# Attention and two MLPs on one core: order of the first weights' loads, sizes of two chunks, time of the second weights' conversion

## Chip, core and metric

The kernel runs on one core of a Trainium2 chip. The metric is the device time of one execution in microseconds. The kernel before takes 964.87 us, the median of three runs from 963.07 to 965.61.

## What is computed

Attention with a few global tokens, and two MLPs behind it, all in float32 as far as the outputs go; the four weight matrices arrive as float64. In short:

```python
k_all = np.concatenate([k_g, k_l], axis=2);  v_all = np.concatenate([v_g, v_l], axis=2)
out_g = np.matmul(sm(scale * np.matmul(q_g, k_all.transpose(0, 1, 3, 2))), v_all)
s_ll  = np.where(np.abs(pos[:, None] - pos[None, :]) <= 32, scale * q_l @ k_l.T, -1e9)
a_l   = sm(np.concatenate([scale * q_l @ k_g.T, s_ll], axis=-1))
out_l = np.matmul(a_l, v_all)
x = np.concatenate([out_g, out_l], axis=2)     # 4 x 8 heads x (32 + 512) x 64 -> (2176, 512)
h = x @ w_in;  g = np.maximum(0.01 * h, h);  x = g @ w_out        # d_ff = 2048
h = x @ w_in2; g = h - np.tanh(h);           out = g @ w_out2     # d_ff = 2048
```

## The kernel before

**Tiles.** The 2176 tokens are cut into five chunks: 512, 512, 512, 256, and 256 with the 128 global tokens (384). An item is one block of 128 of the 2048 hidden features (f, 16 of them) for one chunk. In an item of the first MLP, `mlp1_a` makes h in 12 matmuls, ACT and DVE turn it into g, cut in a high and a low part, and `mlp1_b` adds g's product with the second weights to four PSUM banks (y0 to y3) in 12 more, two items later (`SKEW`). Weights and activations are split so (high, low), and three products replace one.

**Order of items.** n = 0 to 7: chunk 0, f = 0 to 7. n = 8 to 23: chunk 1. n = 24 to 31: chunk 0, f = 8 to 15. n = 32 to 47: chunk 2. n = 48 to 63: chunk 3. n = 64 on: chunk 4, and from about 80 the second MLP, chunk by chunk in `order2`. Since chunk 0 is done in two halves, its partial y goes to DRAM (`yp_dram`) after the first half, is loaded by `y_part` into columns of `xh` and `xl` that are free then, and is added when y leaves PSUM in `mlp1_y`.

**Attention** is cut into 32 steps (one pair of heads of 256 tokens); stage s makes the keys of step s + 1, the scores and softmax of s, transposes s - 1 and multiplies s - 2 by v. Ten stages run before item 0. The others are spread beside items by the table in the main loop (last stage, first and last item): stages 10 to 17 beside n = 0 to 7, 18 to 25 beside 24 to 31, 26 to 29 beside 32 to 47, 30 to 33 beside 48 to 58. A chunk's tokens must have left attention before its first item. k and q are loaded for two steps at a time, a group (`load_kq`, three buffers), and so is v (`load_v`, two buffers); global queries add some work every fourth stage (`gavps`, `vn`, `vg`).

**Weights.** They arrive as float64. `load_w` loads a block (512 KB), `convert_w` makes float32 of it with one ACT operation (L127) and three of DVE, and `split_w` makes the high and low parts. For the first MLP's w_in the raw block has a place of its own (`in_load`, then `in_job`): six loads are traced in the first part, the rest beside n = 0 to 9. w_out goes through two buffers (`out_load`, `out_job`), is stored split in DRAM and fetched again for each chunk (`wo_fetch`, two transfers of 256 KB an item). The second MLP's weights are loaded through the same two raw buffers, converted into one of two buffers `wf`, and stored in DRAM as float32 (`w2_job`, 33 of them for 32 blocks); `w2_at` says beside which item each is due, from `w2_first` = 25 to 47. They come back beside chunk 4.

**What sets the order.** PE's instructions keep the order of the program up to item 78 (`fix`). On the other engines and on the DMA queues a planner puts instructions where it expects them to be ready, by the program's order among those that are. Nearly all DMAs are issued from SP's queue, in one line: an instruction there that waits for a buffer holds back those behind it. ACT and DVE too take their work in line. `tc.issue_after(x)` makes what is traced inside it follow x, where it is on x's own engine or queue, and does nothing else.

Of the kernel before, what the change touches and what calls it, by code (L numbers as in the profile page):

```python
# [21 lines left out]
def kernel(  # L22
# [14 lines left out]
    nc = tc.nc  # L37
# [6 lines left out]
    NF = DFF // 128  # L44
# [5 lines left out]
    NU = NHV * H  # L50
# [26 lines left out]
    xh = [persist.tile([128, ND, n], F32R, name=f"xh{n}") for n in (512, 640)]  # L77
    xl = [persist.tile([128, ND, n], F32R, name=f"xl{n}") for n in (512, 640)]
    ident = persist.tile([128, 128], F32, name="ident")

    yp_dram = dram.tile([128, ND, 512], F32, name="yp")
# [2 lines left out]
    w2i_dram = [dram.tile([128, DM], F32, name=f"w2id{f}") for f in range(NF)]  # L84
    w2o_dram = [dram.tile([128, DM], F32, name=f"w2od{f}") for f in range(NF)]

    halves = [2, 2, 2, 1, 1]
    sizes = [256 * n for n in halves]
    starts = [sum(sizes[:c]) for c in range(5)]
    sizes[4] += B * SG  # L90
    order2 = [0, 1, 2, 4, 3]

    place = [(0, 0), (1, 0), (1, 0), (0, 0), (1, 256)]

    def f32(t):
        return t.bitcast(F32)
# [6 lines left out]
    def load_w(kind, w, f, raw=None):  # L103
        if raw is None:
            raw = mlp.tile([128, DM, 2], I32, tag="wraw", name="wraw", bufs=2)
        wi = w.bitcast(I32)
        if kind == "in":
            src = wi[:, f * 256 : (f + 1) * 256].rearrange("(k p) f -> p k f", p=128)
            dst = raw.rearrange("p (k n) t -> p k (n t)", k=ND)
        else:  # L110
            src = wi[f * 128 : (f + 1) * 128, :]
            dst = raw.rearrange("p n t -> p (n t)")
        nc.sync.dma_start(out=dst, in_=src)
        return raw
# [49 lines left out]
    y_ps = {}  # L164
    anchor = [None]
    last_av = [None]
    last_exp = [None]
    av_n = []

    def mm1(xh_t, xl_t, N, tag="h"):  # L170
# [41 lines left out]
    HF = NF // 2  # L212
# [5 lines left out]
        return f // HF * HF + HF - 1 if c == 0 else NF - 1  # L218

    def y_part():  # L220
        for k, x in enumerate((xh[0], xl[0])):
            nc.sync.dma_start(out=f32(x)[:, :, 256:], in_=yp_dram[:, :, 256 * k : 256 * k + 256])

    def mlp1_b(c, f):
        N = sizes[c]
# [17 lines left out]
    def mlp1_y(c, f):  # L243
        N = sizes[c]
        if f == y_last(c, f):
            for d in range(ND):
                st = mlp.tile([128, 512], F32, tag="yst", name="yst", bufs=2)
                if c == 0 and f == NF - 1:
                    for k, x in enumerate((xh[0], xl[0])):
                        ks = slice(256 * k, 256 * k + 256)  # L250
                        nc.vector.tensor_add(st[:, ks], y_ps[d][:, ks], f32(x)[:, d, 256:])  # L251
                elif d % 2:
                    nc.scalar.activation(st[:, :N], y_ps[d][:, :N], AF.Copy)
                else:
                    nc.vector.tensor_copy(st[:, :N], y_ps[d][:, :N])
                to = yp_dram if f < NF - 1 else y_dram[c]
                nc.sync.dma_start(out=to[:, d, :N], in_=st[:, :N])
# [61 lines left out]
    def load_kq(g):  # L319

        if g >= NU // 4:
            return
        b, a, hs = place_of(g)
        qr = att.tile([128, 2, 4, D], F32, tag="qr", name="qr", bufs=3)
        kr = att.tile([128, 3, 4, D], F32, tag="kr", name="kr", bufs=3)

        keyed(kr, k_l, k_g, b, a, hs, [nc.sync, nc.sync, nc.scalar] if g == 0 else None)
        queue = nc.scalar if g < 2 else nc.sync
        for t in range(2):
            s0 = a * HALF + t * 128  # L330
            queue.dma_start(out=qr[:, t], in_=q_l[b, hs, s0 : s0 + 128, :].rearrange("h s d -> s h d"))
        for k in range(2):
            h2 = slice(2 * k, 2 * k + 2)
            raw_t[2 * g + k] = qr[:, :, h2, :], kr[:, :, h2, :]
# [369 lines left out]
    def in_load():  # L704
        if in_todo:
            f = in_todo.pop(0)
            place = persist.tile([128, DM, 2], I32, tag=f"win{f}", name=f"inraw{f}")
            in_raw.append((f, load_w("in", w1_in, f, place)))

    def out_load():  # L710
        if out_todo:
# [57 lines left out]
        tc.cur_priority = at + max(tc.cur_priority - max(at - n, 0), 0)  # L769

    gtodo = []
    w2_first = 25

    start_tags = ["att0", "att1", "att2", "y0", "y1", "y2", "y3"]
    run_tags = ["att0", "att1", "att2"]
# [74 lines left out]
    if True:  # L850
# [16 lines left out]
        for pp in range(PRE):  # L867
            for op in stage(pp):
                op()
            if pp % 2 == 0:  # L870
                in_load()
            if pp == 0:
                load_kq(2)
            if pp == 1:
                load_v(1)
            if pp >= 2 and pp % 2 == 0:
                in_job()
            if pp == PRE - 2:
                out_load()
                out_load()  # L880
# [9 lines left out]

        beside = {}
        pp = PRE
        for last, n0, n1 in ((17, 0, HF - 1), (25, 3 * HF, 4 * HF - 1), (29, 2 * NF, 3 * NF - 1), (NU // 2 + 1, 3 * NF, 4 * NF - 6)):
            ops = []
            while pp <= last:
                ops += stage(pp)
                pp += 1
            for k, op in enumerate(ops):
                beside.setdefault(n0 + k * (n1 - n0) // len(ops), []).append(op)
# [3 lines left out]
            items.insert(n1 - 2 + 1 + 2 * k, items.pop(n1 + k))  # L903
        w2_at = {}
        for k in range(2 * NF + 1):
            w2_at.setdefault(w2_first + k * (47 - w2_first) // (2 * NF), []).append(k)
        last0 = 9 * NF
        b_at = {}
        for n, (ph, c, f) in enumerate(items):
# [2 lines left out]
        for n in range(len(items) + 8):  # L912
            ph, c, f = items[n] if n < len(items) else (3, 0, 0)
            one = items[n - 1] if 0 < n <= len(items) else (3, 0, 0)
            if ph == 1:
                if n in (0, 2, 4, 6) or HF <= n < 2 * HF:
                    in_job()
                if n < 2 * HF - 2:
                    in_load()
                if 1 <= n <= HF or 2 * HF + 1 <= n <= 3 * HF:  # L920
                    out_job()
                if n == 4 * HF:
                    y_part()
                if c == 4 and f == 0:
                    while gtodo:
# [88 lines left out]
```

## Time and profile before

| | us |
|---|---|
| median of three runs | 964.87 |
| profiled execution | 965.56 |
| its span | 963.8 |
| PE busy | 925.9 |
| DVE busy | 624.5 |
| ACT busy | 536.9 |

The page gives each engine's busy time and, in 40 slices of the span, its busy share in tenths, with PE's granted clock (9 is nearly the full 2.4 GHz; the other level is half of it). A window is a stretch of the span with the busy time of each engine in it. In a timeline, a bracket tells how long the engine was idle before an instruction, and whose end released it. A group gathers instructions of one line and form. "DMA share" is the mean busy share of the core's 16 DMA engines. Digits in names are left out: in_moe_w_in_dram is the w_in of either MLP; loaded as inraw it is the first's, as wraw the second's.

### The profile page before, as it was taken

How to read it: one execution, taken by the hardware profiler on the slowest of the kernel's cores; microseconds unless marked ns; L12 is line 12 of the kernel's file. 1: busy time of each engine (PE TensorE's matmuls, PEld its weight loads, DVE VectorE, ACT ScalarE, POOL GpSimd, SP SyncE). 2: the span in 40 equal slices, each digit the busy share in tenths (PEclk: the TensorE clock that was granted, in tenths of full speed). 3: DMA queues.
4: the chain of work that ended last, by engine and by line, in shares of the span. 5: the costliest groups of instructions: out<-in, count | busy, mean ns of one | idle time of the engine just before them, and what ended most of it. 6: DMA issues, size and time to landing. Idle time of an engine off the chain costs nothing.

```text
span 963.8 us, 15440 instructions
## 1 busy us (share of the span) xinstructions
PE 925.9 (96%) x5436; PEld 771.4 (80%) x5436; DVE 624.5 (65%) x1373; ACT 536.9 (56%) x1223; POOL 36.9 (4%) x67
## 2 busy tenths in 40 slices
PE   7869999999998989999999999999999999999998
PEld 4657778788776767777899999888888888899997
DVE  3864878544564454555313347988888988888886
ACT  5866775443666444444434347656555655655565
POOL 5400000000000000000000000000000000000022
PEclk9998999999999999999999999999999999999999
DMA  7897567445476786787647675001100100010010
GB/s 184 240 278 177 152 187 218 149 167 161 126 212 174 224 280 206 251 254 249 194 143 259 192 235 169 29 1 34 45 1 0 46 21 1 1 45 1 1 34 23
DMA packets 146574, 129.22 MB, mean 134 GB/s; under 512 B 89280, under 2 KB 108736, under 8 KB 146496
## 3 DMA queue, kind: packets, MB, share of 16 engines
q1 hardware_dynamic: 143840, 127.57, 43.7%
q10 hardware_dynamic: 2656, 0.66, 0.3%
q8 instruction: 43, 0.70, 0.3%
q14 instruction: 35, 0.29, 0.1%
HBM read 101.45 MB, written 26.74 MB: 133 GB/s over the span
## 4 chain that ended last, share of the span: by engine, by line
PE 77%; DMA 10%; ACT 4%; DVE 4%; SPq 2%; issue 2%; POOL 0%; ACTq 0%; DVEq 0%
PE h L55 34%; PE o L55 19%; PE y L55 14%; DMA wraw<-in_moe_w_in_dram 3%; PE sps L55 2%; PE ptps L453 2%; PE avps L55 2%; ACT e L423 2%; DMA w2id<-wf 2%; DMA wraw<-in_moe_w_out_dram 2%; PE gavps L55 1%; DMA w2od<-wf 1%; ACT wf L127 1%; PE sgps L55 1%; PE kps L354 1%
## 5 line engine op out<-in xcount | busy, mean ns | idle before, releaser
L55 PE MATMUL h<-xh,win 128*128 128x512 f32 (+2 forms) x1280 | 359.3, 364 | 3.6 <-ACT g L204 3.5
L55 PEld LDWEIGHTS h<-xh,win 128*128 128x128 f32 x1280 | 229.2, 190 | 40.1 <-ACT g L204 6.2
L55 PE MATMUL h<-xl,win 128*128 128x512 f32 (+2 forms) x640 | 230.0, 359 | 0.0
L55 PEld LDWEIGHTS h<-xl,win 128*128 128x128 f32 x640 | 121.3, 190 | 15.7
L55 PE MATMUL y<-gh,woh 128*128 128x512 f32 (+2 forms) x320 | 121.4, 379 | 5.1 <-DVE yst L251 3.7
L206 DVE TENSOR_TENSOR gl<-g,gh 128x512 fp32r<-128x512 f32 (+2 forms) x80 | 48.8, 610 | 114.2 <-ACT gh L205 114.1
L55 PE MATMUL y<-gh,wol 128*128 128x512 f32 (+2 forms) x320 | 115.1, 360 | 0.0
L55 PE MATMUL y<-gl,woh 128*128 128x512 f32 (+2 forms) x320 | 114.4, 361 | 0.0
L55 PE MATMUL o<-wo2l,gh 128*128 128x512 f32 x255 | 99.6, 391 | 0.0
L55 PE MATMUL o<-wo2h,gh 128*128 128x512 f32 x255 | 99.4, 390 | 0.0
L55 PE MATMUL o<-wo2h,gl 128*128 128x512 f32 x255 | 97.7, 390 | 0.0
L633 ACT ACTIVATE u<-h 128x512 f32<-128x512 f32 (+2 forms) x80 | 42.6, 532 | 93.3 <-PE h L55 86.4
L204 ACT ACTIVATE g<-h 128x512 f32<-128x512 f32 (+2 forms) x80 | 42.1, 527 | 60.7 <-PE h L55 60.3
L55 PEld LDWEIGHTS y<-gh,woh 128*128 128x128 f32 x320 | 60.5, 189 | 17.0 <-issue 8.8
L127 ACT ACTIVATE wf<-wraw 128x512 f32<-128x512 f32 x48 | 31.8, 662 | 66.0 <-DMA wraw<-in_moe_w_in_dram 20.6
L658 ACT ACTIVATE gh<-p 128x512 fp32r<-128x512 f32 (+2 forms) x80 | 45.4, 568 | 41.0 <-DVE p L642 41.0
L55 PEld LDWEIGHTS y<-gl,woh 128*128 128x128 f32 x320 | 60.5, 189 | 8.2
L55 PEld LDWEIGHTS y<-gh,wol 128*128 128x128 f32 x320 | 60.8, 190 | 5.7
L639 ACT ACTIVATE u<-u,consts 128x512 f32<-128x512 f32 (+2 forms) x80 | 52.7, 659 | 6.8 <-DVE p L637 4.2
L55 PEld LDWEIGHTS o<-wo2h,gl 128*128 128x128 f32 x255 | 47.9, 188 | 10.1
L659 DVE TENSOR_TENSOR gl<-p,gh 128x512 fp32r<-128x512 f32 (+1 forms) x64 | 41.8, 653 | 21.7 <-ACT gh L658 20.8
L55 PEld LDWEIGHTS o<-wo2h,gh 128*128 128x128 f32 x255 | 47.9, 188 | 9.1
(109 smaller groups left out, 1428.7 us busy)
## 6 DMA issues: line engine op xcount, KB each, us to landing
wraw<-in_moe_w_out_dram SPq DMA_DIRECT2D x32, 512.0 KB, 4.2
woh<-wod SPq DMA_DIRECT2D x64, 256.0 KB, 4.0
wol<-wod SPq DMA_DIRECT2D x64, 256.0 KB, 3.6
inraw<-in_moe_w_in_dram SPq DMA_DIRECT2D x16, 512.0 KB, 6.2
wraw<-in_moe_w_in_dram SPq DMA_DIRECT2D x16, 512.0 KB, 4.8
vr<-in_v_l_dram SPq DMA_DIRECT2D x48, 96.0 KB, 2.8
kr<-in_k_l_dram SPq DMA_DIRECT2D x47, 96.0 KB, 2.9
vn<-in_v_l_dram SPq DMA_DIRECT2D x32, 128.0 KB, 3.3
```

Source lines behind the costliest of these rows:

```text
L55: nc.tensor.matmul(o, lhsT, rhs, start=start, stop=stop)
L127: nc.scalar.activation(w, hw.bitcast(F32), AF.Copy, scale=REBIAS)
L204: nc.scalar.activation(g[:, :N], h[:, :N], AF.Prelu, alpha=0.01)
L206: anchor[0] = nc.vector.tensor_sub(gl[:, :N], g[:, :N], f32(gh)[:, :N])
L354: nc.tensor.transpose(ps[:, c : c + n], kr[:n, t].rearrange("p h d -> p (h d)"), ident[:n, :n])
L423: last_exp[0] = nc.scalar.activation(e[:, h, j, s0 : s0 + n], x, AF.Exp, bias=st[:, k : k + 1], scale=-1.0, accum_out=st[:, 4 + k : 5 + k],)
L453: nc.tensor.transpose(ps[:, k * 128 : (k + 1) * 128], e[:, h, j, c0 : c0 + 128], ident)
L633: nc.scalar.activation(u, h, AF.Square)
L639: nc.scalar.activation(u, u, AF.Square, bias=tc_a2)
L658: nc.scalar.activation(gh[:, :N], p, AF.Copy)
L659: eng["pool" if i == order2[-1] else "dve"].tensor_sub(gl[:, :N], p, f32(gh)[:, :N])
```

## The change

Chunk 2 gets 256 tokens and chunk 3 gets 512; `order2` follows, so that the second MLP still ends with the 256-token chunk. The partial y of chunk 0 is loaded into `xh[1]` and `xl[1]` (columns 256 to 511, which chunk 2 no longer uses) at n = 25, not into `xh[0]` and `xl[0]` at n = 32. Stages 18 to 21 alone stand beside n = 24 to 31, and 22 to 29 beside n = 32 to 47. Each load of w_in follows, on SP, the last q load traced before it (`last_kq`); in the first part they are traced after odd stages instead of even ones, later beside n = 0, 2 and 4 to 11 instead of 0 to 9. The second weights are due from n = 32 to 60 instead of 25 to 47.

```diff
-    halves = [2, 2, 2, 1, 1]
+    halves = [2, 2, 1, 2, 1]
-    order2 = [0, 1, 2, 4, 3]
+    order2 = [0, 1, 3, 4, 2]
+    last_kq = [None]
     def y_part():
-        for k, x in enumerate((xh[0], xl[0])):
-            nc.sync.dma_start(out=f32(x)[:, :, 256:], in_=yp_dram[:, :, 256 * k : 256 * k + 256])
+        for k, x in enumerate((xh[1], xl[1])):
+            nc.sync.dma_start(out=f32(x)[:, :, 256:512], in_=yp_dram[:, :, 256 * k : 256 * k + 256])
...
-                    for k, x in enumerate((xh[0], xl[0])):
+                    for k, x in enumerate((xh[1], xl[1])):
                         ks = slice(256 * k, 256 * k + 256)
-                        nc.vector.tensor_add(st[:, ks], y_ps[d][:, ks], f32(x)[:, d, 256:])
+                        nc.vector.tensor_add(st[:, ks], y_ps[d][:, ks], f32(x)[:, d, 256:512])
...
-            queue.dma_start(out=qr[:, t], in_=q_l[b, hs, s0 : s0 + 128, :].rearrange("h s d -> s h d"))
+            last_kq[0] = queue.dma_start(out=qr[:, t], in_=q_l[b, hs, s0 : s0 + 128, :].rearrange("h s d -> s h d"))
...
-            in_raw.append((f, load_w("in", w1_in, f, place)))
+            with tc.issue_after(last_kq[0].ins):
+                in_raw.append((f, load_w("in", w1_in, f, place)))
...
-    w2_first = 25
+    w2_first = 32
...
-            if pp % 2 == 0:
+            if pp % 2:
                 in_load()
...
-        for last, n0, n1 in ((17, 0, HF - 1), (25, 3 * HF, 4 * HF - 1), (29, 2 * NF, 3 * NF - 1), (NU // 2 + 1, 3 * NF, 4 * NF - 6)):
+        for last, n0, n1 in ((17, 0, HF - 1), (21, 3 * HF, 4 * HF - 1), (29, 2 * NF, 3 * NF - 1), (NU // 2 + 1, 3 * NF, 4 * NF - 6)):
...
-            w2_at.setdefault(w2_first + k * (47 - w2_first) // (2 * NF), []).append(k)
+            w2_at.setdefault(w2_first + k * (60 - w2_first) // (2 * NF), []).append(k)
...
-                if n < 2 * HF - 2:
+                if n in (0, 2) or 4 <= n < 12:
                     in_load()
...
-                if n == 4 * HF:
+                if n == 3 * HF + 1:
                     y_part()
```

## Rows read from the trace of the kernel before

**Rows 1.** The page: span, PE's sum, PE and its clock in 40 slices of 24.1 us.

```profile
span 963.8 us, 15440 instructions
...
PE 925.9 (96%) x5436; PEld 771.4 (80%) x5436; DVE 624.5 (65%) x1373; ACT 536.9 (56%) x1223; POOL 36.9 (4%) x67
...
PE   7869999999998989999999999999999999999998
...
PEclk9998999999999999999999999999999999999999
```

**Rows 2.** Windows (from:to us): length, then busy us of each engine, clock, DMA share, GB/s.

```profile
core 0: us, PE busy (x) PEld busy (x) DVE busy (x) ACT busy (x) POOL busy (x), PEclk, DMA share, GB/s
59.70:81.10 21.40, 12.72 (x103) 9.95 (x101) 10.21 (x32) 11.46 (x32) 0.00 (x0) 0.76 0.84 236
81.10:152.30 71.20, 70.51 (x522) 53.53 (x521) 54.09 (x169) 54.22 (x148) 0.30 (x2) 1.00 0.68 183
176.40:236.20 59.80, 59.80 (x265) 49.55 (x264) 26.98 (x44) 22.49 (x37) 0.00 (x0) 1.00 0.51 167
241.70:334.20 92.50, 86.95 (x603) 65.72 (x602) 47.75 (x169) 54.78 (x153) 0.31 (x2) 0.96 0.63 182
285.60:334.20 48.60, 43.50 (x306) 33.62 (x306) 24.34 (x82) 26.48 (x73) 0.00 (x0) 0.93 0.65 194
334.20:349.40 15.20, 15.20 (x105) 12.02 (x104) 10.22 (x29) 7.33 (x19) 0.00 (x0) 1.00 0.88 283
349.40:367.30 17.90, 14.17 (x62) 11.30 (x61) 7.84 (x17) 6.41 (x13) 0.00 (x0) 0.90 0.79 249
367.30:450.10 82.80, 79.81 (x409) 61.85 (x407) 44.97 (x109) 36.11 (x82) 0.30 (x2) 1.00 0.75 241
334.20:450.10 115.90, 109.19 (x573) 85.17 (x571) 63.03 (x155) 49.85 (x112) 0.30 (x2) 0.99 0.78 247
503.70:512.40 8.70, 8.70 (x75) 8.70 (x74) 2.52 (x5) 2.92 (x7) 0.00 (x0) 1.00 0.66 212
```

**Rows 3.** Timeline of SP's queue around item 0 (start us, us, engine line op tiles).

```profile
50.66 3.84 SPq L113 DMA_DIRECT2D inraw<-in_moe_w_in_dram  x5
...
55.87 5.76 SPq L113 DMA_DIRECT2D inraw<-in_moe_w_in_dram  x5
...
61.72 1.22 SPq L315 DMA_DIRECT2D vr<-in_v_l_dram  x1
```

**Rows 4.** Timeline of PE around item 0; in brackets idle us before and its releaser.

```profile
56.95 0.94 PE L55 MATMUL avps<-pt,vr 128*64 128x128 f32 x16
...
70.19 2.05 PE L55 MATMUL avps<-pt,vr 128*64 128x128 f32 x16 [4.65 <-DMA vr<-in_v_g_dram]
...
75.48 0.42 PE L55 MATMUL gavps<-pg,vg 32*64 32x32 f32 x4 [1.49 <-DMA vg<-in_v_g_dram]
```

**Rows 5.** The same of DVE.

```profile
68.64 1.04 DVE L442 TENSOR_SCALAR e<-e,st 128x192 f32<-128x192 f32 x4
```

**Rows 6.** Timelines of PE and ACT in items 28 to 35: instructions that waited.

```profile
293.33 1.56 PE L55 MATMUL sps<-kt,qt 64*128 64x224 f32 x8 [1.49 <-ACT kt L356]
...
313.04 0.66 PE L453 MATMUL ptps<-ident,e 128*128 128x128 f32 x4 [1.32 <-DVE xl L485]
...
325.16 1.12 PE L453 MATMUL ptps<-ident,e 128*128 128x128 f32 x4 [2.28 <-DVE xl L485]
...
358.48 0.47 PE L55 MATMUL y<-gh,woh 128*128 128x512 f32 x1 [3.73 <-DVE yst L251]
...
291.77 0.66 ACT L127 ACTIVATE wf<-wraw 128x512 f32<-128x512 f32 x1 [1.70 <-DMA w2id<-wf]
...
319.38 0.68 ACT L127 ACTIVATE wf<-wraw 128x512 f32<-128x512 f32 x1 [3.92 <-DMA w2od<-wf]
```

**Rows 7.** Groups by form, L127: count, busy us, mean ns, idle before; 241.7:334.2, then 367.3:450.1.

```profile
L127 ACT ACTIVATE wf<-wraw 128x512 f32<-128x512 f32 x9 | 6.0, 663 | 11.1 <-DMA w2od<-wf 3.9 <-DMA kr<-in_k_l_dram 2.0 <-DMA wraw<-in_moe_w_out_dram 1.7
...
L127 ACT ACTIVATE wf<-wraw 128x512 f32<-128x512 f32 x16 | 10.7, 666 | 38.3 <-DMA wraw<-in_moe_w_in_dram 13.9 <-DMA w2od<-wf 7.5 <-DMA wraw<-in_moe_w_out_dram 6.9
```

## The prediction

> **What bounds the kernel now.** I read four views, in this order.
>
> First the page: TensorE (PE) is busy 925.9 of 963.8 us, and its slices are full almost everywhere; the dents stand in the first quarter and in slices 12 to 15, and the granted clock falls in the first few slices and near the middle of the span [rows 1]. So nothing is to be won but PE's stalls, and the time that it runs at the lower of its two clock levels (1.2 instead of 2.4 GHz).
>
> Then the windows [rows 2], cut where the h matmuls, counted in dozens, begin a new item. Undisturbed, eleven 512-token items take 59.8 us, 5.44 us each, and three 256-token items 8.7 us, 2.9 us each. The stalls before the second MLP are four:
> - item 0 (59.7 to 81.1 us): 8.7 us of 21.4 idle, clock 0.76;
> - items 24 to 31 (241.7 to 334.2), where eight attention stages stand beside eight items: idle 92.5 - 86.95 = 5.5 us, and the clock of 0.93 in the 48.6 us from 285.6 on means another 3.4 us lost; 8.9 in sum;
> - the hand-over of the y banks from chunk 0 to chunk 2 (349.4 to 367.3): idle 3.7, clock 0.90 of 17.9 us, 1.8 lost; 5.5 in sum;
> - items 36 to 47 (367.3 to 450.1): idle 82.8 - 79.81 = 3.0 us.
>
> Then who ended them. In item 0, PE's attention matmuls (avps) waited 4.65 us until 70.19 for a load of v, and the global ones (gavps) 1.49 us for another [rows 4]. Why that load was late stands in SP's queue: ten loads of first weights went out in two runs of five from 50.66 us on, and the load of v only behind them, at 61.72 [rows 3]. In items 24 to 31 the PE waits name ACT's kt or DVE's xl, but in front of two of them ACT itself sat 1.70 and 3.92 us before a conversion of second weights (L127), until the stores had freed its buffers [rows 6]. ACT takes its work in order, so such a wait holds up whatever attention has behind it.
>
> Last, L127 as a group [rows 7]: beside the dense attention of items 24 to 31 there are 9 conversions with 11.1 us of ACT idle before them; in 367.3 to 450.1 there are 16, with 38.3. The latter cost PE only 3.0 us. A waiting conversion is cheap where PE has MLP matmuls and dear where attention is dense.
>
> **The change, part by part.** No instruction is added or removed. The sizes of chunks 2 and 3 are swapped, so the 512-, 384- and 256-token items are as many as before, in both MLPs, and the last chunk of the second MLP still has 256 tokens. All of the effect is order.
>
> *First weights behind attention's loads.* Each load of first weights now follows, on SP, the last q load traced before it. The first one gets no edge, since that q load is on ACT's queue. The ten of [rows 3] come apart: one behind the q loads of group 7, one behind 8, two behind 10, six behind 11. Of the six traced ahead of item 0 the last two now stand behind groups 6 and 7. The v load that came late is then behind one load of weights instead of ten. Item 0 loses its 4.65 and 1.49 us of waits, and the low clock after them: about 7.4 us of work ran at half speed from 70.19 on (the 16 avps matmuls took 2.05 us there, 0.94 at 56.95), so 3.7 us. That is 9.8. But PE would then reach the transposes at about 68.6, and DVE finishes their input only at 69.7 [rows 4, 5], so 1.1 to 1.5 us come back as a wait. I take 8.5 off; the ends are 6.1 (clock falls anyway) and 9.8. What is late next is that softmax.
>
> The six loads behind group 11 go out in one run, near item 5. The ten of before landed some 1.4 us apart (two runs, 50.66 to 61.6, with v arriving at 70), so the run of six holds the DMA for 8 us. Queued behind it are loads of the other first weights and v loads with two stages (some 20 us) to spare. From 81.1 to 152.3 the DMA share is 0.68 and PE idles 0.7 us [rows 2], so there is room; I add 1 us, ends 0 and 4.
>
> *Half the attention in items 24 to 31, and no second weights there.* Four stages instead of eight stand beside these items and no conversion does. The cause of the 8.9 us is gone; the cover is 5.44 us of MLP for every half stage. From 81.1 to 152.3 the same dense attention, with ACT 54.2 of 71.2 us busy and loads that come in time, idles PE only 0.7 us [rows 2]. I leave 0.5: -8.4. Loading the partial y moves to item 25, two 512 KB transfers into a part of xh and xl that chunk 1 has left; what is queued behind it on SP are loads for stages later by several us, so nothing.
>
> *The hand-over to chunk 2.* Its cause, two staging buffers that wait for their stores, stays, but the w2 stream has only begun when it comes, where before the DMA share was 0.88 just ahead of it [rows 2]; on the other hand the cover is a 256-token item. I leave 2.0 of 5.5: -3.5. The like hand-over from chunk 3 to 4 is now 512 tokens wide: +0.5 (between 0 and the 3.7 of [rows 6]).
>
> *Items 36 to 47 of before* lose their 3.0 us with their conversions.
>
> *Chunk 2, the new dense place.* Sixteen 256-token items get eight attention stages and, counting the new schedule of due items (32 + 28k/32), 18 of the 32 conversions. PE needs 16 x 2.9 = 46.4, plus 2.5 for two second-layer items of chunk 0 that run here at 512 tokens, plus 8 stages. A stage costs (92.5 - 8.9 - 8 x 5.44) / 8 = 5.0 us by items 24 to 31, so 89 us in all. What is to be added is PE's loss to waiting conversions, which the trace doesn't show at this density. Three ways to size it:
> - per conversion, as in items 24 to 31: 8.9 / 9 = 1.0 us, clock included; 18 of them cost 18 us;
> - by transfers: 19 loads of 512 KB, 18 stores and 32 fetches of 256 KB, four groups of k, q and v (about 960 KB each) and some 2 MB of v and y make 29 MB. At the best rate of a stage, 283 GB/s at a share of 0.88, that takes 103 us, a loss of 14. At the rate of 334.2 to 450.1 as a whole (247 GB/s, share 0.78) it takes 118, a loss of 29 [rows 2]. With the DMA engines never idle (247 / 0.78 = 317 GB/s) it takes 92, a loss of 3;
> - per conversion as in items 36 to 47, 3.0 / 16 = 0.19 us: 3.4.
>
> I take 18, as the row of the same kind of attention has it, and it lies between the transfers' two rates; ends 3 and 29.
>
> *Chunk 3* has 512-token items, four last stages and the 14 other conversions, as items 36 to 47 have now: 14 x 0.19 = 2.6, ends 0 and 14 (at 1.0 each). The last conversion is due at item 60, and the second weights are needed from 64 on: nothing, with three items of 5.4 us or more as cover.
>
> **A rule against it.** What the row shows is that early loads did harm: ten at once put v behind them [rows 3]. The Trainium skill, "DMA: Bandwidth & Descriptors", section "Rules for kernel authors", says the opposite of the edit: issue a DMA early, compute, and wait for it late. By that rule item 0 gains nothing and the six late weights make ACT wait as second weights do. Its price is worked out under the third rival; the trace speaks for the rule with second weights (ACT waits for them) and against it with first weights.
>
> **The sum.** -8.5 + 1.0 - 8.4 - 3.5 + 0.5 - 3.0 + 18.0 + 2.6 = -1.3 us. The profiled execution took 965.56 us (a span of 963.8 and 1.8 around it), so 964.3. The median of the runs lies 0.7 lower, so 963.5 us, 0.14% under the median of before. A measurement of this kernel tells about 0.3%, 2.9 us, from no change.
>
> **Rivals.**
> - *Transfers keep up.* The loss in chunk 2 is 3 to 12 us instead of 18: 948 to 958. For it: late conversions on a queue that is already waiting overlap, and 16 of them cost PE 3.0 us in all [rows 2, 7]. Against: there the cover was 5.44 us of MLP an item, here 2.9, with half a stage in it. Midpoint 954.
> - *Second weights bound chunk 2* (slower). Each conversion waits for a load into one of two buffers and for a store out of one of two. If ACT waits 2.4 us for each, as in items 36 to 47 (38.3 / 16), 18 of them make 43 us, of which the dense attention covers little: a loss of 25 to 36 us, and so 971 to 982. It decides from a loss of about 22 us on. For it: 29 MB in 89 us would be 327 GB/s, which no row of [rows 2] reaches. Against: waits in the dense place averaged 1.2 us (11.1 / 9).
> - *First weights come too late, or v is held up elsewhere.* The gain of 8.5 is lost, in whole or in part, or six late conversions wait 1.2 us each: 963.5 + 8.5 = 972, up to 979. Against: the weights of f = 8 are first used in item 16, and each of the ten conversions stands four items or more behind its load.
> - The change may also not do what it says: the edge orders SP's queue alone, so a run of loads can still form behind any q load. That is the run of six, and is in the third rival's price.
>
> **How the numbers follow.** Forecast (a loss of 12 to 24 us in chunk 2, 957 to 970): 0.47, of which 0.13 faster, 0.22 the same, 0.12 slower. Transfers keep up: 0.25, faster. Second weights bound chunk 2: 0.20, slower. First weights too late: 0.08, of which 0.03 the same and 0.05 slower. So faster 0.38, same 0.25, slower 0.37. The range is 950 to 977: it takes in most of both rivals, leaving about 0.1 on either side; the likeliest case alone has 957 to 970.
>
> **What would show it.** In the trace of the changed kernel: v loads issued within some 5 us of the q loads of group 6, and item 0 about 13 us long at full clock; items 24 to 31 in some 64 us without idle; chunk 2's sixteen items in some 107 us (not 89, not 118), with ACT idle before L127 and half-clock stretches in it, and the DMA share over 0.8; chunk 3 in about 103. The prediction is wrong if chunk 2 runs near 90 or near 120 us, if a load of first weights ends a PE or ACT wait in items 1 to 12, or if stalls appear after item 64, where I expect none that differ.

## The result

The kernel after takes 952.72 us (median of four runs, 951.32 to 956.66), the one before 963.97 beside it (960.69 to 965.61): a ratio of 0.9894, 95% interval 0.9853 to 0.9935. It is 1.1% faster, where 0.14% was forecast. The time lies inside the range of 950 to 977, but not in the likeliest case (957 to 970); it is the rival "Transfers keep up" (948 to 958), whose loss of 3 to 12 us in chunk 2 the profiled execution has: 9.1 against a run without second weights (w2_none, below), 10.7 against the prediction's 89. The profiled execution, the slowest of the four, took 956.66 us with a span of 954.9.

The page of after, to be laid beside [rows 1] (span, busy sums, PE and its granted clock in 40 slices):

```profile
span 954.9 us, 15444 instructions
...
PE 924.7 (97%) x5436; PEld 774.2 (81%) x5436; DVE 624.8 (65%) x1373; ACT 539.4 (56%) x1223; POOL 37.0 (4%) x67
...
PE   7889999999999989979999999999999999999998
...
PEclk9999999999999998989999999999999999999999
```

PE does the same work. The dent of the first quarter is shallower, and those of slices 12 to 15 have moved to slices 15 to 18, where chunks 2 and 3 now stand with the attention and the conversions.

Windows of after, one for each stage, with the columns of [rows 2]; the last three are short stretches behind a stall of PE, for the section on the hardware:

```profile
core 0: us, PE busy (x) PEld busy (x) DVE busy (x) ACT busy (x) POOL busy (x), PEclk, DMA share, GB/s
59.60:73.00 13.40, 10.86 (x103) 8.30 (x101) 9.55 (x32) 10.64 (x31) 0.00 (x0) 0.87 0.85 214
73.00:233.60 160.60, 158.91 (x925) 126.20 (x924) 102.45 (x248) 93.49 (x214) 0.30 (x2) 1.00 0.65 201
233.60:295.20 61.60, 61.60 (x361) 47.83 (x360) 20.71 (x75) 31.12 (x78) 0.30 (x2) 1.00 0.43 129
295.20:394.90 99.70, 93.56 (x816) 82.60 (x815) 61.69 (x204) 59.25 (x172) 0.30 (x2) 0.95 0.80 244
394.90:503.40 108.50, 103.16 (x593) 83.94 (x592) 51.11 (x113) 47.12 (x96) 0.00 (x0) 0.97 0.72 232
...
341.20:344.60 3.40, 3.40 (x18) 3.31 (x16) 0.59 (x3) 1.28 (x2) 0.00 (x0) 0.50 0.90 292
361.80:368.50 6.70, 6.70 (x37) 5.26 (x37) 4.29 (x18) 3.05 (x11) 0.00 (x0) 0.50 0.63 212
409.50:416.20 6.70, 4.31 (x16) 3.83 (x17) 4.38 (x11) 3.01 (x8) 0.00 (x0) 0.50 0.57 176
```

Put in a table, with the stages of before cut at the same items, and with what the forecast amounts to for each stage: the lengths it gave as signs, 161.6 for items 1 to 23 with the six late loads, and 109 for chunk 2 with the 2.0 us left of the hand-over.

| stage (us) | before | forecast | after |
|---|---|---|---|
| item 0 | 21.4 | 13 | 13.4 |
| items 1 to 23 | 160.6 | 161.6 | 160.6 |
| items 24 to 31 | 92.5 | 64 | 61.6 |
| items 32 to 47 (chunk 2) | 115.9 | 109 | 99.7 |
| items 48 to 63 (chunk 3) | 65.2 | 103 | 108.5 |
| item 64 to the end | 448.5 | 448.5 | 451.5 |

The last row is no stall: PE's idle time there is 4.6 us, against 4.9 before. The second-layer halves of a chunk's last two items run behind the next chunk's first h; chunk 3 now has 512 tokens, so they are 2 x (5.44 - 2.9) / 2 = 2.5 us longer, an estimate from the item lengths of [rows 2]. The forecast overlooked that.

SP's queue around item 0 (start us, us, engine, line, operation, tiles, count), where [rows 3] had runs of five loads:

```profile
48.77 0.95 SPq L332 DMA_DIRECT2D qr<-in_q_l_dram  x2
49.76 0.51 SPq L113 DMA_DIRECT2D inraw<-in_moe_w_in_dram  x1
...
50.91 0.39 SPq L316 DMA_DIRECT2D vr<-in_v_l_dram  x1
...
59.82 1.10 SPq L113 DMA_DIRECT2D inraw<-in_moe_w_in_dram  x2
```

One load of weights stands behind the q loads of group 6, and the v load of [rows 3], there at 61.72, follows at 50.91. Timeline of PE of the kernel after, around item 0 and then in chunks 2 and 3 (in brackets idle us before and its releaser):

```profile
63.36 0.44 PE L364 MATMUL qps<-ident,qr 128*128 128x128 f32 x2 [2.54 <-ACT pg L569]
...
65.89 2.05 PE L55 MATMUL avps<-pt,vr 128*64 128x128 f32 x16
...
68.94 0.30 PE L55 MATMUL gavps<-pg,vg 32*64 32x32 f32 x4
...
340.30 0.28 PE L575 MATMUL gt2ps<-ident,sg 128*32 128x128 f32 x1 [2.78 <-DVE xl L486]
...
361.77 1.75 PE L55 MATMUL sps<-kt,qt 64*128 64x192 f32 x6 [1.77 <-ACT kt L357]
...
411.89 0.40 PE L575 MATMUL gt2ps<-ident,sg 128*32 128x128 f32 x1 [5.24 <-DVE xl L486]
```

The 4.65 and 1.49 us of [rows 4] are gone. The wait of 2.54 us, which names ACT, is not new. The kernel before has it too, in a line that [rows 4] leaves out:

```profile
63.50 0.44 PE L363 MATMUL qps<-ident,qr 128*128 128x128 f32 x2 [2.54 <-ACT pg L568]
```

There the clock was still 1.00 in the 2 us behind it, and then PE waited for v. In after the clock is 0.52 from 65.9 to 68.2 us, so the 16 avps matmuls still take 2.05 us, not 0.94. From item 24 to item 63 only the waits before 340.30, 361.77 and 411.89 are longer than 1 us. The hand-over's 3.73 us of [rows 6] (yst) has no successor.

What stands behind the wait at 411.89 is on ACT and DVE; their timelines of after, from 4 us into chunk 3 on:

```profile
399.00 0.67 ACT L127 ACTIVATE wf<-wraw 128x512 f32<-128x512 f32 x1 [4.53 <-DMA wraw<-in_moe_w_in_dram]
...
402.19 0.66 ACT L127 ACTIVATE wf<-wraw 128x512 f32<-128x512 f32 x1 [1.41 <-DMA w2od<-wf]
...
399.70 0.43 DVE L128 TENSOR_SCALAR wt<-wf 128x512 int32<-128x512 int32 x1 [4.77 <-ACT wf L127]
400.16 0.69 DVE L132 SCALAR_TENSOR_TENSOR wt<-wraw,wt 128x512 int32<-128x512 int32 x1
400.89 0.69 DVE L135 SCALAR_TENSOR_TENSOR wf<-wraw,wt 128x512 int32<-128x512 int32 x1
...
402.88 0.43 DVE L128 TENSOR_SCALAR wt<-wf 128x512 int32<-128x512 int32 x1 [1.30 <-ACT wf L127]
...
411.42 0.41 DVE L486 TENSOR_TENSOR xl<-avps,xh 128x256 fp32r<-128x256 f32 x1
```

ACT sits before a conversion until a load lands, and DVE sits before the conversion's second step until ACT has made the first. Softmax and xl stand behind them in the same two lines, and PE waits for xl at 411.89. The conversions take time of these engines too: 0.67 us of ACT and 0.43 + 0.69 + 0.69 = 1.8 of DVE each, and three of them stand in chunk 3 ahead of this xl. That the conversions are the cause shows where they are left out (w2_none, below): there the same wait is 0.18 us, and gt2ps starts 11.2 us into the chunk instead of 17.0. How much of that is their waits and how much their own work, no run separates. The groups of L127, chunk 2 and then chunk 3 (count, busy us, mean ns, idle before), beside [rows 7]:

```profile
L127 ACT ACTIVATE wf<-wraw 128x512 f32<-128x512 f32 x14 | 9.4, 671 | 11.4 <-DMA wraw<-in_moe_w_in_dram 4.6 <-DMA wraw<-in_moe_w_out_dram 4.2 <-DMA w2od<-wf 2.6
...
L127 ACT ACTIVATE wf<-wraw 128x512 f32<-128x512 f32 x16 | 10.7, 669 | 27.0 <-DMA wraw<-in_moe_w_in_dram 12.7 <-DMA wraw<-in_moe_w_out_dram 8.6 <-DMA w2od<-wf 3.4
```

Chunk 2 got 14 conversions, not 18, and chunk 3 got 16, not 14. Two of the 32 ran ahead of item 32 (at 228.81 and 243.81), since a due item is no earliest time, and two slid into the next chunk.

### The profile page after: what moved, and what is told of

It reads as the page before. It is cut to its first block, busy times and chain, and to the rows that moved or that the text cites. A ratio compares the mean times of both kernels' runs of the same rounds, so it can differ in the third digit from the quotient of the medians.

```text
span 954.9 us, 15444 instructions
## 1 busy us (share of the span) xinstructions
PE 924.7 (97%) x5436; PEld 774.2 (81%) x5436; DVE 624.8 (65%) x1373; ACT 539.4 (56%) x1223; POOL 37.0 (4%) x67
## 4 chain that ended last, share of the span: by engine, by line
PE 82%; DMA 8%; ACT 4%; DVE 4%; issue 1%; SPq 1%; POOL 0%; ACTq 0%; DVEq 0%
PE h L55 34%; PE o L55 19%; PE y L55 16%; PE sps L55 3%; DMA wf<-w2id 3%; PE avps L55 3%; DMA wraw<-in_moe_w_in_dram 3%; PE ptps L454 2%; DMA wf<-w2od 2%; ACT e L424 1%; PE sgps L55 1%; PE gavps L55 1%; PE kps L355 1%; ACT win L141 1%; DVE win L142 1%
## 5 line engine op out<-in xcount | busy, mean ns | idle before, releaser
L55 PEld LDWEIGHTS y<-gh,woh 128*128 128x128 f32 x320 | 60.9, 190 | 13.4 <-issue 5.0
L127 ACT ACTIVATE wf<-wraw 128x512 f32<-128x512 f32 x48 | 31.9, 665 | 45.9 <-DMA wraw<-in_moe_w_in_dram 17.3
L55 PEld LDWEIGHTS o<-wo2h,gl 128*128 128x128 f32 x255 | 47.8, 188 | 10.1
L660 DVE TENSOR_TENSOR gl<-p,gh 128x512 fp32r<-128x512 f32 (+1 forms) x64 | 41.8, 653 | 21.5 <-ACT gh L659 21.4
L55 PEld LDWEIGHTS o<-wo2l,gh 128*128 128x128 f32 x255 | 47.9, 188 | 9.0
```

The source lines that it names most:

```text
L55: nc.tensor.matmul(o, lhsT, rhs, start=start, stop=stop)
L127: nc.scalar.activation(w, hw.bitcast(F32), AF.Copy, scale=REBIAS)
L660: eng["pool" if i == order2[-1] else "dve"].tensor_sub(gl[:, :N], p, f32(gh)[:, :N])
```

## Experiments

In each a ratio is to the kernel before, run beside it. "Loss" is a stage's length less that of the same stage in w2_none, which has no second weights at all. Columns of all rows are those of the same view above.

**The loads alone.** The kernel before with the new edge and the new places of the loads of first weights:

```diff
+    last_kq = [None]
...
-            queue.dma_start(out=qr[:, t], ...)
+            last_kq[0] = queue.dma_start(out=qr[:, t], ...)
...
-            in_raw.append((f, load_w("in", w1_in, f, place)))
+            with tc.issue_after(last_kq[0].ins):
+                in_raw.append((f, load_w("in", w1_in, f, place)))
...
-            if pp % 2 == 0:
+            if pp % 2:
...
-                if n < 2 * HF - 2:
+                if n in (0, 2) or 4 <= n < 12:
```

> The kernel before with the edge behind the q loads and the new places of the first weights' loads, and nothing else. Theory (the two halves of the change add up): item 0 shrinks from 21.4 to about 13.4 us, everything from item 1 on stays, so some 8 us less than before (ratio about 0.992). Rival (the gain needs the swapped chunks, or the weights are late without them): item 0 gains less than 3 us, or items 1 to 15 lose what it gains; ratio 0.997 or more.

It takes 956.16 us against 964.53, ratio 0.9903 (0.9866 to 0.994). Item 0 in its windows:

```profile
59.80:73.20 13.40, 10.86 (x104) 8.31 (x101) 9.52 (x32) 10.65 (x31) 0.00 (x0) 0.87 0.83 206
```

Items 1 to 23 take 160.6 us as before, and items 24 to 31 keep their stalls (91.9 us). So the first weights alone are worth 8.4 us, 8.0 of them in item 0 of the profiled execution.

**The edge alone.** As above, with the places of before:

> The kernel before with the edge behind the last q load and the old places of the loads. Theory (the edge is what spreads the loads; their places in the program hardly matter): item 0 at 12 to 14 us, some 8 us less than before, as with edge and places together. Rival (the places matter as much): item 0 loses 4 us or more of that gain.

955.59 us against 965.29, ratio 0.9899 (0.9864 to 0.9934), and the same 13.4 us for item 0. SP's queue has the order of the run before: one load of weights behind the q loads at 48.35, v at 51.28, two loads at 59.51. The edge does it; the spreading adds nothing that can be measured. The places without the edge were not tried.

**The rest without the loads.** The kernel after with the loads as they were:

```diff
-            with tc.issue_after(last_kq[0].ins):
-                in_raw.append((f, load_w("in", w1_in, f, place)))
+            in_raw.append((f, load_w("in", w1_in, f, place)))
...
-            if pp % 2:
+            if pp % 2 == 0:
...
-                if n in (0, 2) or 4 <= n < 12:
+                if n < 2 * HF - 2:
```

> The changed kernel with the first weights' loads as before (no edge, old places). Theory: item 0 is 21 us long again, with the wait for v, and the rest is as in the changed kernel, so about 8 us more than the changed kernel and 3 less than before (ratio to before about 0.997). Rival (the wait for v went for another reason): item 0 stays near 13 us, ratio 0.989.

961.97 us (ten runs) against 964.53, ratio 0.9968 (0.9942 to 0.9994). PE's timeline around item 0 has the old waits again:

```profile
69.87 1.79 PE L55 MATMUL avps<-pt,vr 128*64 128x128 f32 x16 [2.60 <-DMA vr<-in_v_g_dram]
...
75.25 0.43 PE L55 MATMUL gavps<-pg,vg 32*64 32x32 f32 x4 [1.87 <-DMA vg<-in_v_g_dram]
```

Chunk sizes, stages and second weights together are worth 2.6 us (0.6 to 5.6 by the interval); with the 8.4 of the loads that makes 11.0, and the whole change measured 11.2. So the two parts add up, as far as this noise lets one tell.

**The second weights later, alone.** The kernel before with its conversions due at items 32 to 60:

```diff
-    w2_first = 25
+    w2_first = 32
...
-            w2_at.setdefault(w2_first + k * (47 - w2_first) // (2 * NF), []).append(k)
+            w2_at.setdefault(w2_first + k * (60 - w2_first) // (2 * NF), []).append(k)
```

> The kernel before with the second weights due from item 32 to 60 and nothing else. Theory (conversions of second weights stall the dense attention): items 24 to 31 lose their 8.9 us of idle and low clock, items 32 to 47 keep about what they have, items 48 to 60 with 256 tokens and 14 conversions gain up to 5 us of stalls; 4 to 8 us less than before (ratio 0.992 to 0.996). Rival (dense attention stalls by itself, by its own loads and chains): items 24 to 31 keep 6 us or more of their loss, ratio 0.998 to 1.003.

966.08 us (ten runs), ratio 1.0016 (0.9995 to 1.0037): no gain. The windows of items 24 to 31, of chunk 3 and of all from item 64 on:

```profile
241.80:324.40 82.60, 82.60 (x604) 63.17 (x603) 33.99 (x142) 50.65 (x145) 0.31 (x2) 1.00 0.47 127
...
433.80:505.30 71.50, 66.08 (x593) 61.44 (x593) 39.40 (x100) 33.75 (x88) 0.00 (x0) 0.98 0.87 291
505.30:964.20 458.90, 447.53 (x2185) 389.00 (x2184) 348.29 (x629) 259.90 (x497) 11.86 (x16) 0.99 0.19 62
```

And the timelines of PE and ACT early in the last of them:

```profile
521.61 1.52 PE L55 MATMUL h<-xh,win 128*128 128x512 f32 x2 [5.20 <-ACT win L141]
...
520.92 0.63 ACT L141 ACTIVATE win<-wf 128x512 fp32r<-128x512 f32 x1 [3.79 <-DMA wf<-w2id]
```

Eight stages beside items 24 to 31 idle PE not at all when one conversion stands among them (at 252.87 us) instead of nine: 82.6 us instead of 92.5. So the conversions were the cause of that stall, and not the dense attention. Items 32 to 47, with 15 conversions instead of 22, gain another 6.5 (109.4 for 115.9). But all of it is given back: 6.3 us in the short chunk 3, where 14 conversions now stand, and 10.4 from item 64 on, where the second weights come back too late for PE. The theory's total, 4 to 8 us less, was missed. After has conversions as late and loses nothing from item 64 on; that its 512-token chunk 3, with 16 items of 5.44 us or more instead of 2.9, is what allows it is argued, not shown alone.

**The second weights early in the new kernel.** After, with the due items of before (25 to 47): the same two lines, the other way round.

> The changed kernel with the second weights due from item 25 to 47 as before. Theory (each conversion beside dense attention costs some 0.6 us, one beside a half-dense 512-token item little): items 24 to 31 lose 2 us, chunk 2 with 22 conversions loses 14 instead of 11, chunk 3 without any loses about 1 instead of 9; within 4 us of the changed kernel. Rival (the later start is what makes the change gain): 6 us or more above the changed kernel.

955.43 us, ratio 0.9898 (0.9858 to 0.9937), within 3 us of after. The group of L127 in items 24 to 31, where four stages now stand:

```profile
L127 ACT ACTIVATE wf<-wraw 128x512 f32<-128x512 f32 x8 | 5.4, 674 | 14.5 <-DMA wraw<-in_moe_w_in_dram 6.3 <-DMA w2id<-wf 2.7 <-DMA w2od<-wf 2.3
```

ACT waits more before eight conversions (14.5 us) than it did before nine in [rows 7] (11.1), and yet these items take 62.0 us, 0.4 more than after. What was dear at a stage an item is free at half a stage an item. So moving half of the attention away is enough to free items 24 to 31, and the later start was not needed for it, though it is enough too (w2_late_only). The total came as expected, but not the stages: chunk 2 lost 10.3 us with 18 conversions (14 expected), and chunk 3 lost 5.4 with the five that slid into it (1 expected).

**No second weights.** After without their loads, conversions and stores; when they should come back, blocks of q are fetched in their place.

```diff
-            w2_raw.append((kind, f, load_w(kind, w2_in if kind == "in" else w2_out, f)))
...
-        nc.sync.dma_start(out=t, in_=src)
+        nc.sync.dma_start(
+            out=t.rearrange("p (h x) -> p h x", h=2),
+            in_=q_l[b // 4, 2 * (b % 4) : 2 * (b % 4) + 2].rearrange("h (p a) d -> p h (a d)", p=128),
+        )
```

> The changed kernel without any work on the second weights: they are neither loaded, converted nor stored, and what comes back for them beside chunk 4 is a block of q of the same size, so the output is not the reference's. Theory (what chunks 2 and 3 still lose, 20 us in the profiled execution, is conversions that wait in line on ACT and DVE): items 32 to 63 lose 3 us or less, about 16 us less than the changed kernel, ratio to before about 0.972. Rival (dense attention stalls by itself): items 32 to 63 still lose 10 us or more, ratio 0.98 or more.

941.28 us (940.65 to 941.61). Windows of chunks 2 and 3:

```profile
295.20:385.80 90.60, 87.55 (x815) 78.11 (x814) 36.27 (x156) 51.95 (x158) 0.30 (x2) 1.00 0.52 158
385.80:486.50 100.70, 100.52 (x593) 82.10 (x592) 24.88 (x65) 37.22 (x80) 0.00 (x0) 1.00 0.31 106
```

And PE's timeline in them:

```profile
338.90 0.28 PE L575 MATMUL gt2ps<-ident,sg 128*32 128x128 f32 x1 [1.50 <-DVE xl L486]
...
397.02 0.28 PE L575 MATMUL gt2ps<-ident,sg 128*32 128x128 f32 x1 [0.18 <-DVE xl L486]
```

The second weights cost 952.72 - 941.28 = 11.4 us in all, 0.36 us for each conversion; in the profiled execution it is 9.1 us in chunk 2 and 7.8 in chunk 3. Without them PE idles 3.2 us in items 32 to 63, about the 3 of the theory, where after has 11.5; so dense attention by itself is not the stall. (The 16 us expected in all are the distance from the profiled execution of after.) The rows show more: the transposes for the global queries (gt2ps) have no slack even here, for they wait 1.50 and 0.18 us. These are the two places where after waits 2.78 and 5.24.

**The transfers without the conversions.** Loads and stores of after, of the same sizes, with nothing computed between them:

```diff
-            with tc.issue_after(anchor[0].ins):
-                w = convert_w(raw)
-            later.append(lambda: nc.sync.dma_start(out=dst, in_=w))
+            later.append(lambda: nc.sync.dma_start(
+                out=dst.rearrange("p (a n) -> p a n", a=4), in_=ident.unsqueeze(1).to_broadcast([128, 4, 128])
+            ))
```

> The changed kernel with the second weights' loads and stores of the same sizes, but without their conversion on ACT and DVE; what is stored is a constant block, so the output is not the reference's. Theory (waits in line on ACT and DVE cost, not the transfers): within 4 us of the kernel without any of it. Rival (the transfers crowd out what attention and the fetches need): items 32 to 63 lose 10 us or more, within 6 us of the changed kernel.

956.42 us, ratio 0.9909 (0.9885 to 0.9933), and inconclusive on the question. With nothing to wait for, the planner sent the stores from 38.5 us on, into item 0 and the items behind it: item 0 took 17.1 us, with a wait of 2.22 for vg, and items 1 to 23 took 166.8. Chunk 2 lost 4.1 us and chunk 3 nothing. A second version ties every load and store on SP behind the last fetch of w_out:

```diff
+            def store():
+                with tc.issue_after(last_fetch[0].ins):
+                    nc.sync.dma_start(out=dst.rearrange(...), in_=ident.unsqueeze(1).to_broadcast([128, 4, 128]))
+            later.append(store)
...
+            with tc.issue_after(last_fetch[0].ins):
+                w2_raw.append((kind, f, load_w(kind, w2_in if kind == "in" else w2_out, f)))
```

> The changed kernel with the second weights' loads and stores but without their conversion, as once before, and now each load and store is tied to follow the last fetch of the first MLP's second weights on SP, so that they go out beside items 32 to 60, where the changed kernel has them. What is stored is a constant block, so the output is not the reference's. Theory (in-line waits for conversions cost, transfers as such hardly do): chunk 2 at 91 to 94 us and chunk 3 at 101 to 102, within 4 us of the kernel without second weights (941). Rival (transfers crowd out attention's loads and fetches): chunk 2 at 97 us or more, the whole within 6 us of the changed kernel.

939.52 us (938.37 to 940.27), no slower than without any second weights. Windows of chunks 2 and 3:

```profile
294.10:384.40 90.30, 87.69 (x816) 78.21 (x816) 36.32 (x156) 51.95 (x158) 0.30 (x2) 1.00 0.91 277
384.40:485.50 101.10, 100.73 (x592) 81.94 (x592) 24.80 (x65) 36.99 (x80) 0.00 (x0) 1.00 0.81 254
```

Chunk 2 moves 277 GB/s x 90.3 us = 25.0 MB, as after does (244 x 99.7 = 24.3), at a share of 0.91, and PE idles no more than in w2_none. The DMA engines were no bound. What costs is the conversions in the lines of ACT and DVE: their waits for what the DMA moves, and their own work.

**The first step on GpSimd.** After, with L127's operation on POOL for the second weights:

```diff
-        nc.scalar.activation(w, hw.bitcast(F32), AF.Copy, scale=REBIAS)
+        if on_pool:
+            nc.gpsimd.tensor_scalar(out=w, in0=hw.bitcast(F32), scalar1=REBIAS, scalar2=None, op0=ALU.mult)
+        else:
+            nc.scalar.activation(w, hw.bitcast(F32), AF.Copy, scale=REBIAS)
...
-                w = convert_w(raw)
+                w = convert_w(raw, True)
```

> The changed kernel with the first step of each second weight's conversion, which waits for its load, on GpSimd instead of ACT; the three DVE steps stay. Theory: ACT no longer waits for loads and has 0.66 us less to do per conversion; DVE still waits in line for the first step. Half of the loss of items 32 to 63 goes, 6 to 10 us less than the changed kernel. Rival (DVE's wait alone stalls attention as much): within 3 us of the changed kernel.

946.09 us (943.91 to 951.03), ratio 0.981 (0.9774 to 0.9846). The group of that line in chunk 2:

```profile
L128 POOL TENSOR_SCALAR wf<-wraw 128x512 f32<-128x512 f32 x14 | 22.4, 1599 | 88.5 <-DMA wraw<-in_moe_w_in_dram 42.3 <-DMA wraw<-in_moe_w_out_dram 14.5 <-DVE st L436 12.8
```

The step takes 1.60 us there instead of 0.67, and its engine sits idle for 88.5 us before it; but hardly anything else stands in that line (two operations of 0.15 us in chunk 2). It gives back 6.6 of the 11.4 us. The loss is 3.5 us in chunk 2 and 3.2 in chunk 3. What is left in chunk 3 is the wait for DVE's xl:

```profile
402.58 0.28 PE L578 MATMUL gt2ps<-ident,sg 128*32 128x128 f32 x1 [3.31 <-DVE xl L489]
```

Ahead of that xl, DVE sat 4.49 us until POOL had made a first step, and took seven steps of conversions, 4.0 us. That it would go if DVE were spared too is argued, not shown.

**A wider stretch.** After, due from item 24 to 60 instead of 32 to 60 (`w2_first = 24`):

> The changed kernel with the second weights due from item 24 to 60 instead of 32 to 60: some 15 conversions instead of 18 in chunk 2, 7 beside items 24 to 31, which idle 0 us now. Theory (a conversion beside half-dense 512-token items is nearly free, one in chunk 2 costs 0.6 us): 1 to 4 us less than the changed kernel. Rival (conversions stall wherever there is attention): the same or more.

947.6 us (947.46 to 948.42), ratio 0.982 (0.9798 to 0.9842), 5.1 under after and more than the 1 to 4 expected. The groups of L127 in items 24 to 31, chunk 2 and chunk 3:

```profile
L127 ACT ACTIVATE wf<-wraw 128x512 f32<-128x512 f32 x6 | 4.0, 675 | 9.3 <-DMA wraw<-in_moe_w_in_dram 5.0 <-DVE st L417 1.7 <-DVE wol L142 1.6
L127 ACT ACTIVATE wf<-wraw 128x512 f32<-128x512 f32 x13 | 8.8, 676 | 15.9 <-DMA wraw<-in_moe_w_out_dram 11.0 <-DMA wraw<-in_moe_w_in_dram 3.7 <-DMA vr<-in_v_l_dram 0.6
L127 ACT ACTIVATE wf<-wraw 128x512 f32<-128x512 f32 x12 | 8.0, 670 | 21.1 <-DMA wraw<-in_moe_w_in_dram 13.2 <-DMA wraw<-in_moe_w_out_dram 7.9
```

They take 61.6, 93.7 and 105.5 us: a loss of 0, 3.1 and 4.8. Thirteen conversions cost 3.1 us in the chunk where fourteen cost after 9.1, with more idle of ACT before them (15.9 against 11.4).

**Around the dense chunk.** After, with 16 due beside items 24 to 31, none beside chunk 2 and 17 beside chunk 3:

```diff
-            w2_at.setdefault(w2_first + k * (60 - w2_first) // (2 * NF), []).append(k)
+            w2_at.setdefault(24 + k // 2 if k < 16 else 48 + (k - 16) * 13 // 17, []).append(k)
```

> The changed kernel with 16 of the second weights' jobs due beside items 24 to 31, none beside chunk 2, and 17 beside items 48 to 60. Theory (a conversion costs PE where attention is dense): chunk 2 loses about 3 us, as without second weights, items 24 to 31 lose 0 to 2, chunk 3 5 to 8; 4 to 8 us less than the changed kernel. Rival (a conversion costs the same wherever it stands): the 16 cost items 24 to 31 some 9 us, and the whole is within 3 us of the changed kernel.

949.91 us (948.5 to 951.59), ratio 0.9834 (0.9792 to 0.9875). The groups of L127 in the same three stages:

```profile
L127 ACT ACTIVATE wf<-wraw 128x512 f32<-128x512 f32 x12 | 8.0, 664 | 20.9 <-DMA w2od<-wf 10.5 <-DMA wraw<-in_moe_w_in_dram 9.4 <-DVE wol L142 1.0
L127 ACT ACTIVATE wf<-wraw 128x512 f32<-128x512 f32 x4 | 2.7, 669 | 4.3 <-DMA w2od<-wf 2.7 <-DMA wraw<-in_moe_w_in_dram 1.7
L127 ACT ACTIVATE wf<-wraw 128x512 f32<-128x512 f32 x15 | 10.0, 668 | 33.7 <-DMA wraw<-in_moe_w_out_dram 11.4 <-DMA w2od<-wf 10.5 <-DMA wraw<-in_moe_w_in_dram 9.4
```

They take 67.4, 94.4 and 102.0 us: a loss of 5.8, 3.8 and 1.3. Twelve beside half-dense attention cost 5.8, where eight cost 0.4; fifteen in chunk 3 cost 1.3, with 33.7 us of ACT idle, where sixteen cost after 7.8. Sparing the dense chunk gains something there and gives most of it back beside items 24 to 31. The whole is 2.8 us under after, so the theory's 4 to 8 was missed.

PE's wait for the first gt2ps of chunk 3, here and in w2_24_60 and w2_early:

```profile
408.02 0.29 PE L575 MATMUL gt2ps<-ident,sg 128*32 128x128 f32 x1 [1.36 <-DVE xl L486]
...
403.82 0.29 PE L575 MATMUL gt2ps<-ident,sg 128*32 128x128 f32 x1 [3.43 <-DVE xl L486]
...
409.92 0.31 PE L575 MATMUL gt2ps<-ident,sg 128*32 128x128 f32 x1 [2.72 <-DVE xl L486]
```

In each run this is nearly all of PE's idle time in chunk 3, and the loss goes roughly with it and not with the number of conversions in the chunk:

| chunk 3 of | wait for xl (us) | loss (us) | conversions |
|---|---|---|---|
| w2_none | 0.18 | 0 | 0 |
| w2_around | 1.36 | 1.3 | 15 |
| w2_pool | 3.31 | 3.2 | 16 |
| w2_24_60 | 3.43 | 4.8 | 12 |
| w2_early | 2.72 | 5.4 | 5 |
| after | 5.24 | 7.8 | 16 |

What differs is what stands ahead of that one xl: in w2_around two conversions, and DVE waited for neither; in after three, with the waits shown above. This is read from the profiled executions; no run tests it alone.

**GpSimd and the wider stretch together.** Both edits:

> The changed kernel with the first step of each second weight's conversion on GpSimd, and the second weights due from item 24 to 60: the two that each beat the changed kernel (946.1 and 947.6 us) together. Theory (both take from the same loss of 11 us that second weights still cost): 943 to 946 us. Rival (their gains add up): 941 us or less.

947.79 us (942.85 to 953.37), ratio 0.9814 (0.9761 to 0.9867): no better than either alone, and outside both the theory and the rival. Its chunks 2 and 3 take 91.1 and 105.6 us in the profiled execution, which is the fastest of its four. The gains don't add; why not stays open.

These last four versions all have medians under that of after; in two of them, GpSimd and the wider stretch, every run lies under the fastest of after (951.32). The wider stretch is the smallest edit (one number) with four runs inside 1.0 us; GpSimd has the lowest median.

## Where the prediction was right and where wrong

Right:
- *The views*: the four stalls were the ones that moved. The late v loads as the cause in item 0 and the conversions as the cause in items 24 to 31 are each confirmed by an experiment that changes them alone (edge_only, w2_late_only).
- *Item 0*: -8.5 forecast, 21.4 - 13.4 = -8.0 in the trace, -8.4 by medians. The size was in part luck. The prediction took back 1.1 to 1.5 us for a wait for the softmax of [rows 5], which did not come, and expected full clock. What cost instead is the clock of 0.87, 13.4 x 0.13 = 1.7 us, behind the old wait of 2.54 us, which the prediction counted in its 8.7 of idle but did not name.
- *Items 24 to 31*: no idle, 61.6 us for 64.
- No first weight ends a wait in items 1 to 12; the third rival is out. The run of six loads did form, from 126.29 us on with one load of v in it, and cost nothing, not 1 us.
- *The rule against it.* Loading the first weights later, behind attention's loads, is worth 8.4 us (loads_only) and 9.7 (edge_only). The Trainium skill, "DMA: Bandwidth & Descriptors", section "Rules for kernel authors", says to issue early and wait late; for first weights the trace disagrees, as the queue is one line and early loads made the urgent ones late. For second weights an earlier start with the same end (w2_24_60) is worth 5.1 us, as the rule would have it, though it also thins the conversions in chunk 2; the earliest of all (w2_transfers) harmed item 0.

Wrong:
- *The term for the conversions in chunks 2 and 3, +18.0 and +2.6.* This is the step that failed. Its count was taken as the due items (18 and 14 instead of 14 and 16), and its price from two groups of [rows 7]. The profiled execution shows 9.1 / 14 = 0.65 us each in chunk 2 instead of 1.0, and 7.8 / 16 = 0.49 in chunk 3 instead of 0.19; together 16.9 for 20.6, and 11.4 by medians. A price for each conversion is the wrong measure altogether. The runs have 0.05 us each (eight beside items 24 to 31 in w2_early), 0.09 (fifteen in chunk 3 in w2_around), 1.1 (five in chunk 3 in w2_early) and 1.2 (eight of the nine in [rows 7], by w2_late_only's 9.9 us), and the idle time of ACT doesn't follow it either. The loss goes by how much the conversions delay an operation for which PE has no slack. In chunk 3 of after that is one place: gt2ps, 17 us into the chunk, 5.24 us of its 5.3 of idle.
- *By transfers*, as a bound of that term (3, 14 and 29 us). The same bytes without conversions cost nothing, at 277 GB/s and a share of 0.91. A rate seen in a stage that itself waits is no limit; it is what the waits left over. The bytes were too many as well: 29 MB, where chunk 2 moved 24.3. The rival "Second weights bound chunk 2" rested on this too.
- *The hand-overs*, 2.0 and 0.5 left: nothing was left of either. The reason given, a stream of second weights that has only begun, is not enough: in w2_late_only it begins as late, and PE still waits 3.26 us for yst there, until 348.18. Why the wait went with the swapped chunks stays open.
- *The sum* had -1.3 us; the profiled executions differ by 956.66 - 965.56 = -8.9, a gap of 7.6. The stage lengths given as signs didn't agree with the sum: in the table they make 899.1 against 904.1 before, so -5.0, of which 2.5 is the work that moves behind item 64. Adding them up would have shown it. Against those lengths chunk 2 came out 9.3 us shorter, items 24 to 31 2.4 and items 1 to 23 1.0, while chunk 3 was 5.5 longer, the rest behind it 3.0 and item 0 0.4. The other 3.2 us up to the medians (963.5 to 952.7) come from the profiled executions: after's is 3.9 over its median, before's was 0.7 over its own.

## What to carry over

A load that nobody needs yet can be the dearest one on an in-order queue: tie it behind the urgent ones and leave it there. Price what is added to the line of an in-order engine, its waits and its work, neither by its length nor by the number of instructions, but by how much it delays the operation behind it for which the busiest engine has no slack; look for the places where that engine waits a little even without the disturbance. And before a transfer rate bounds a forecast, make sure that the stretch it was read in was waiting for transfers and not for the engines that feed them.

## What the runs showed of the hardware

PE's granted clock fell to the lower level (1.2 GHz) behind some of its waits and not behind others of the same length. In the windows of after the clock is 0.50 for 3.4 us behind the wait of 2.78 us, for 6.7 behind 1.77, and for 6.7 around the end of 5.24. In w2_24_60 waits of 1.46 and 1.90 us in chunk 2 left it at 1.00. The same wait of 2.5 us in item 0 was followed by the low clock in after, loads_only and edge_only (13.4 us for the item) but not in w2_early, w2_pool and w2_transfers_due (12.1 us), so a stage with the same loads and waits differs by 1.3 us from run to run.

The spread of a kernel's runs does not simply go with the waits. w2_none, with the fewest, stays within 1.0 us over four runs, after has 5.3, and no_loads 10.1 over ten; but w2_24_60, with waits of up to 3.43 us, stays within 1.0 too, while w2_pool, with waits of up to 3.31, has 7.1 and w2_pool_24_60, with 3.62, has 10.5. That the clock behind the stalls makes this spread is argued, not shown.
